# Pooled attention and a gated convolution FFN on one core: masks, fillers, q loads, conv buffers, one batch's pooling and the queue order changed together

## The chip, the cores and the metric

The kernel runs on one core of a Trainium2 chip, in one launch. The metric is the device time in microseconds; for one core this is the time of that core. A profile is taken of one execution, whose own time and span are given below beside the times of the unprofiled runs.

## The reference

Inputs are q, k and v of 8 batches, 8 heads, 576 positions and 64 channels, and the weights of a feed-forward block. k and v are averaged over groups of 8 neighbouring positions, so that each of the 576 queries attends to 72 keys. The attention output, 8 x 64 = 512 channels wide, goes through a projection to 1024 channels, a ReLU, a convolution over three neighbouring positions per channel, a sigmoid gate, and a projection back to 512.

```python
k_p = k.reshape(B, H, Sp, pool, D).mean(axis=3)      # pool = 8, Sp = 72
v_p = v.reshape(B, H, Sp, pool, D).mean(axis=3)
scores = scale * np.matmul(q, k_p.transpose(0, 1, 3, 2))
attn = softmax(scores)
x = np.matmul(attn, v_p)                             # then heads side by side: 8 x 576 x 512
h = np.maximum(x @ w_in, 0.0)                        # 512 -> 1024
conv_out[s] = sum(conv_w[k] * h[s + k - 1] for k in range(3))
gate = 1.0 / (1.0 + np.exp(-conv_out))
out = (h * gate) @ w_out                             # 1024 -> 512
```

## The kernel before

Everything is computed in bf16 with sums in PSUM in f32. The inputs are f32 in memory and are cast by the transfers that load them; all loads are issued from GpSimd (POOL), all stores and the load of the small convolution weights from SyncE (SP).

The work is cut into operations. Each `pl.add(name, engine, duration, fn, ...)` records one: its name, its engine, an estimated duration, the function that issues its instructions, what it reads and writes, and the PSUM slot that it takes or gives back. When all are recorded, `order()` simulates the engines with these estimates and emits the operations in the order of that simulation: at each step it takes the operation that can start first, and among those that an engine could start within 0.02 us of each other the one with the lowest rank. The ranks are a list of integers, `PARAMS["prio"]`, one for each operation in the order in which the operations are recorded. So an engine's order of instructions is fixed when the kernel is built, and an instruction that waits holds back all behind it on that engine; POOL's loads are in that order too. `PARAMS["act"]` names the copies that go to ScalarE (ACT); those not named go to VectorE (DVE).

The operations of batch b, in the order of the data:

- `ldk`, `ldv`, `ldq`: the loads (L440 and L444 for k, L460 and L465 for v, L410 for q). k, v and q have two buffers each, by batch. A row of k_b holds the 8 neighbouring positions of one pooled position, 512 elements.
- `kp1`, `kp2`, `ksum` and `vp1`, `vp2`, `va` (L593, L600, L610, L642): the pooling on DVE, each step adding the two halves of what is left. `vb` (L646, L651) multiplies the pooled v by a mask, which places each head's rows, into `vblk`.
- `qg` (L420): two copies for each batch that regroup q by head pairs. `qT` (L664) transposes q on PE, `qTe` (L670) copies it out of PSUM; `kT` and `kz` (L623, L630) do the same for the pooled k.
- `sc` (L690, L692) the scores, `exp` (L698) their exponential on ACT, `av` (L715, L719) the product with `vblk`, `rc` and `nm` (L728, L732) the division, `xt` (L746) the transpose and `xte` (L752) the copy to `xT`.
- `mm1` (L766 for batch 0, in two parts; L789 for the others) and `relu` (L773, L795): the projection to 1024 channels, in 8 blocks `f` of 128.
- The convolution, for two blocks at a time: mostly on DVE and ACT (`cp0` and `cp2`, L835 on ACT or L837 on DVE, then `ca0` L844 and `ca2` L854), with `cv` as its buffer, of which there are two; five blocks take it on PE (L912) with the diagonal weights `dw` (L562). `tanh` (L862, L919) is the gate, `g` (L900) the product.
- `mm2` (L943) the projection to 512, for pairs of batches in 9 tiles of 128 rows; `oe` (L966) copies a tile out and `st` stores it.

Where the simulation has PE idle in the first 60 us, `warm` (L382) puts filler matmuls on a tile of zeros into the gap, with a count that follows from the gap's simulated length.

Constants come first: `zero` (L483) is the operand of the fillers, `ident` the identity, `mask` the mask for `vb`. Its columns 8 to 12 are built by nine memsets on DVE (L552 to L555), the rest by one memset and two selects on POOL (L542, L547).

Of the kernel before, what the change touches and what calls it, by code (L numbers as in the profile page):

```python
# [17 lines left out]
        "8 1 5 16 3 9 18 19 20 21 56 30 24 23 12 22 37 66 2 185 123 108 153 106 121 104 90 43 "  # L18
        "27 78 117 97 87 114 14 6 77 41 7 11 46 53 0 10 17 29 25 4 13 31 45 51 60 64 107 174 "
        "32 34 50 67 71 55 15 42 35 40 26 38 49 58 48 52 44 47 59 62 69 74 54 73 75 33 63 36 "  # L20
        "57 28 82 61 65 39 86 91 116 88 89 83 100 126 95 92 80 98 99 94 96 70 105 133 76 85 101 112 "
        "140 109 113 93 81 79 72 154 160 164 170 179 175 142 125 137 178 150 161 171 176 68 183 200 202 205 204 184 "
        "190 193 199 201 191 197 203 186 195 207 189 194 221 224 208 210 215 219 216 209 222 225 230 228 226 180 235 243 "
        "242 220 231 236 239 245 115 144 130 134 102 111 136 139 146 156 147 165 172 181 206 227 234 249 84 110 127 128 "
        "120 119 129 118 122 135 132 138 141 151 232 217 246 241 157 163 124 103 145 148 155 158 223 247 196 192 260 264 "
        "280 288 292 298 131 143 152 149 162 167 168 169 238 211 166 182 248 257 261 266 237 240 302 319 341 336 338 327 "
        "370 340 356 382 173 159 198 187 253 314 269 273 301 324 188 213 233 258 218 252 214 229 177 272 281 287 321 290 "
        "365 345 339 335 368 362 354 361 350 347 353 379 387 400 394 381 377 406 389 415 390 395 398 407 420 405 410 414 "
        "421 358 416 422 408 433 441 268 275 262 267 300 299 283 276 285 284 305 303 317 250 254 274 278 265 293 296 308 "
        "279 304 297 329 325 342 244 251 255 271 294 270 315 330 323 331 328 306 349 291 295 282 289 322 316 311 320 344 "  # L30
        "357 380 403 401 418 424 435 442 492 499 496 509 517 518 536 545 561 565 259 256 286 277 326 334 337 359 366 369 "
        "307 309 310 367 318 263 312 348 212 346 351 364 376 372 363 375 402 436 393 360 411 417 355 374 423 431 439 446 "
        "447 444 451 457 511 524 481 487 471 542 546 495 504 466 533 534 513 527 532 539 540 456 467 464 475 488 483 470 "
        "480 460 501 506 510 529 538 440 445 453 459 450 469 458 465 474 482 485 491 505 512 530 544 490 497 560 568 515 "
        "551 520 555 570 592 593 502 521 476 473 526 503 525 486 535 543 553 537 548 541 595 605 603 621 636 627 635 657 "
        "673 666 333 332 352 343 388 396 399 404 413 412 371 385 373 384 378 392 386 391 313 425 427 430 434 429 549 563 "
        "419 426 550 556 516 522 437 443 581 597 596 650 633 615 634 639 655 661 652 659 662 674 677 654 663 669 679 683 "
        "658 675 670 684 685 554 557 572 589 579 588 569 598 587 591 583 614 628 625 564 578 574 586 590 599 566 607 609 "
        "626 638 623 653 688 646 664 584 602 667 642 671 616 681 693 707 698 710 717 601 594 608 618 645 637 651 644 640 "
        "613 660 665 705 714 720 731 730 740 750 760 770 765 771 782 787 802 798 397 409 432 428 454 507 478 484 479 489 "  # L40
        "438 452 449 448 462 461 472 468 383 494 498 508 519 571 604 612 641 648 624 629 528 531 622 631 734 737 739 747 "
        "767 749 758 761 757 775 756 764 772 786 791 769 776 779 785 790 778 792 795 797 801 702 703 643 699 715 711 701 "
        "718 721 713 722 727 743 746 694 700 692 695 708 704 732 725 723 741 733 736 748 806 735 744 729 742 763 738 751 "
        "754 777 783 788 781 809 841 709 716 712 719 753 752 745 762 766 768 774 773 799 832 826 854 842 870 856 861 871 "
        "892 816 907 493 463 500 477 547 552 559 582 585 610 523 514 619 630 558 576 567 575 455 562 577 573 728 690 755 "
        "759 724 726 682 689 672 678 676 668 805 811 813 838 844 840 845 846 873 875 859 864 867 879 887 794 869 865 878 "
        "883 881 882 888 898 902 822 828 815 820 851 818 827 821 831 807 857 843 872 880 804 810 808 814 812 819 825 824 "
        "780 829 833 836 850 848 876 885 852 860 884 868 891 866 905 894 912 917 918 928 817 823 834 839 835 853 830 847 "
        "855 862 901 890 927 910 924 935 939 923 963 944 965 954 996 1006 1018 1032 1038 600 611 617 680 686 697 580 606 649 "
        "656 687 691 632 647 620 696 706 796 793 837 849 858 863 784 789 874 877 800 803 886 895 899 938 949 889 893 896 "  # L50
        "900 903 897 906 911 962 970 941 945 948 956 959 951 958 961 952 969 916 922 921 925 932 930 929 946 934 971 950 "
        "942 960 968 908 914 904 909 915 931 919 920 926 936 940 937 947 953 976 974 913 933 987 957 978 943 980 991 989 "
        "995 998 1002 966 972 955 964 988 984 993 986 994 1016 1003 1017 1023 1025 1027 1036 1034 1044 1047 1039 1040 1052 1055 1056 967 "
        "975 979 982 997 1010 1045 992 1009 1014 1083 1019 1030 1026 1013 1021 973 977 1046 1054 983 1005 990 999 1012 1053 1051 1007 1015 "
        "981 1004 1031 1029 1020 1033 1037 1041 1048 1043 1042 1050 1001 1011 985 1008 1057 1049 1022 1000 1024 1028 1035 1060 1058 1059 1062 1065 "
        "1066 1061 1063 1068 1067 1071 1064 1073 1070 1069 1072 1075 1076 1074 1077 1078 1079 1081 1080 1082 "
# [6 lines left out]
        "kz.0.0 qTe.0.1 qTe.0.3 xte.0.0 xte.0.3 kz.1.1 qTe.1.0 qTe.1.1 xte.1.0 xte.1.1 xte.1.2 xte.1.3 "  # L63
        "xte.1.4 cp0.0.0 cp0.0.1 cp0.0.2 cp0.0.5 cp0.0.6 cp2.0.7 oe.0.0 oe.0.1 oe.0.2 oe.0.3 kz.2.0 "
        "kz.2.1 qTe.2.0 qTe.2.1 xte.2.0 xte.2.2 xte.2.3 xte.2.4 cp2.1.2 cp0.1.7 cp2.1.7 oe.0.4 oe.0.5 "
        "oe.0.6 oe.0.7 oe.0.8 qTe.3.1 qTe.3.2 xte.3.0 xte.3.1 xte.3.2 xte.3.3 xte.3.4 cp0.2.1 cp2.2.2 "
        "cp0.2.5 cp0.2.6 cp0.2.7 cp2.2.7 oe.1.0 oe.1.1 oe.1.2 oe.1.3 kz.4.0 kz.4.1 qTe.4.1 qTe.4.2 "
        "xte.4.0 xte.4.1 xte.4.3 cp0.3.1 cp2.3.1 cp0.3.3 cp2.3.2 cp2.3.7 oe.1.5 oe.1.6 oe.1.7 qTe.5.0 "
        "qTe.5.1 qTe.5.2 xte.5.0 xte.5.2 cp2.4.0 cp2.4.1 cp2.4.3 cp0.4.4 cp0.4.6 oe.2.2 oe.2.3 kz.6.1 "
        "qTe.6.1 xte.6.3 cp0.5.0 cp0.5.2 cp2.5.2 cp0.5.4 cp0.5.5 cp0.5.6 cp0.5.7 cp2.5.7 oe.2.4 oe.2.5 "  # L70
        "oe.2.6 kz.7.0 qTe.7.0 qTe.7.1 xte.7.2 xte.7.3 cp0.6.0 cp2.6.0 cp0.6.3 cp2.6.3 cp0.6.4 oe.3.0 "
        "oe.3.1 oe.3.2 cp0.7.0 cp0.7.3 cp0.7.5 oe.3.5 oe.3.6 oe.3.7 oe.3.8.0 "
# [5 lines left out]
    "acc": [0, 0, 0, 0, 0, 0, 0, 0],  # L78
    "ncv": 2,
# [203 lines left out]
def packets(n, nbytes, cast=True):  # L283
    return n / 16, 0.022 + 0.000074 * nbytes if cast else 0.006 + 0.000038 * nbytes
# [3 lines left out]
def kernel(  # L288
# [86 lines left out]
    def warm(gap, x):  # L375
        n = min(int((gap - 0.05) / 0.06), 100)
        if x is not None:
            t = pp.tile([P, 2 if x[0] == "A" else 1, 512], FP32, name=f"psw{x[0]}", tag=f"ps{x[0]}{x[1]}")[:, 0, 0:P]
        else:
            return  # L380
        for _ in range(n):
            nc.tensor.matmul(out=t, lhsT=zero[:, 0:P], rhs=zero[:, 0:P], start=True, stop=True)  # L382
# [14 lines left out]
    def load_q(b, prio):  # L397
# [6 lines left out]
        n = 2 if b == 0 else 1  # L404
        for x in range(n):
            c = slice(x * H // n, (x + 1) * H // n)
            ys = (x,) if n > 1 else (0, 1)

            def fn(e, c=c):
                nc.gpsimd.dma_start(out=q_b[b % NQ][:, c].rearrange("p h i d -> p h (i d)"), in_=rows_q(b)[:, c, :])  # L410
            pr = prio + (PARAMS["ld0"][x] if b == 0 else 0.0)
            pl.add(f"ldq{b}.{x}", "POOL", 0.8, fn, writes=[("ql", b % NQ, y) for y in ys], prio=pr, dma=packets(PR * H // n, 1024))
# [68 lines left out]
    def consts():  # L481
        def fn(e):
            nc.vector.memset(zero, 0.0)  # L483
        zi = pl.add("zero", "DVE", 0.15, fn, writes=["zero"], prio=-80)

        def fn(e):
            make_identity(nc, ident)
# [581 lines left out]
```

## Time and profile before

| | |
|---|---|
| median of the runs | 212.78 us |
| lowest and highest of 3 runs | 212.31 and 214.05 us |
| the profiled execution | 214.0 us, span 212.3 us |
| mean granted clock of PE | 0.992 |
| PE busy, with fillers | 199.2 us |
| fillers on PE (L382) | 19.3 us |
| DVE busy | 181.3 us |
| ACT busy | 174.2 us |
| POOL busy | 45.2 us |
| loads issued from POOL | 16.80 MB in bf16 |

The busy time of an engine is the time in which it executes; the share is taken of the span, from the first instruction to the last. The time of an execution is a little longer than its span. The transfers of a queue run on 16 DMA engines; "landing" is the time from a transfer's issue until its data is there. Idle time that the profile gives to a releaser ended when that releaser finished.

### The profile page before, as it was taken

What the parts mean: (1) busy time and instruction counts of PE and PEld (TensorE: products, weight loads), DVE (VectorE), ACT (ScalarE), POOL (GpSimd) and SP (SyncE); (2) the same over time, 40 slices, a digit from 0 to 9 for tenths busy, and PEclk for the clock granted to TensorE, in tenths of its full rate; (3) what the DMA queues carried; (4) which work ended last, traced back from release to release, by engine and by line L of the source; (5) the groups of instructions that cost most, each with busy time, mean ns of one, the idle gap of its engine ahead of it and who ended that gap; (6) DMA issues with size and microseconds to landing.
All of it is one profiled execution on the core that took longest, in us unless ns stands there. A gap on an engine that the chain in (4) does not pass through costs nothing.

```text
span 212.3 us, 4770 instructions
## 1 busy us (share of the span) xinstructions
PE 199.2 (94%) x1900; PEld 136.7 (64%) x1900; DVE 181.3 (85%) x419; ACT 174.2 (82%) x297; POOL 45.2 (21%) x73
## 2 busy tenths in 40 slices
PE   3999996979997799999999999999999999999993
PEld 3997784857753557756865676756656847764541
DVE  5446889899999999999999999999999978997510
ACT  2017388999999988999999999988999998998412
POOL 7695299602233223130000000000000000000000
PEclk9999999799999999999999999999999999999999
DMA  4999999999999999999302020122020203002344
GB/s 59 178 197 205 207 198 202 203 207 172 199 159 202 227 223 159 221 137 176 114 3 98 5 99 0 54 99 99 3 98 1 102 32 116 3 2 99 147 154 148
DMA packets 26363, 26.56 MB, mean 125 GB/s; under 512 B 5708, under 2 KB 21348, under 8 KB 26340
## 3 DMA queue, kind: packets, MB, share of 16 engines
q0 software_dynamic: 21200, 16.80, 50.8%
q1 hardware_dynamic: 5140, 9.45, 11.8%
q8 instruction: 15, 0.25, 0.4%
q14 instruction: 8, 0.07, 0.1%
HBM read 33.57 MB, written 9.44 MB: 203 GB/s over the span
## 4 chain that ended last, share of the span: by engine, by line
PE 76%; DVE 14%; ACT 6%; issue 2%
PE psfB L943 25%; PE psfA L789 22%; PE pswA L382 6%; PE psfA L715 4%; PE psfA L690 3%; PE psbB L746 3%; PE psbB L664 2%; PE pswB L382 2%; DVE cv L837 2%; PE psfA L719 2%; DVE cv L844 2%; ACT tg L862 2%; DVE p L593 1%; ACT hT L795 1%; DVE cv L854 1%
## 5 line engine op out<-in xcount | busy, mean ns | idle before, releaser
L943 PE MATMUL psfB<-w_out,gT 128*128 128x512 bf16 (+1 forms) x282 | 65.2, 377 | 0.0
L789 PE MATMUL psfA<-xT,w_in 128*128 128x288 bf16 x448 | 59.7, 286 | 0.7 <-ACT xT L752 0.7
L789 PEld LDWEIGHTS <-w_in 128*128 128x128 bf16 x448 | 42.4, 98 | 12.8 <-issue 0.9
L943 PEld LDWEIGHTS <-gT 128*128 128x128 bf16 x290 | 27.7, 98 | 28.8 <-issue 0.3
L795 ACT ACTIVATE hT<-psfA 128x576 bf16<-128x576 f32 x56 | 35.8, 665 | 2.8 <-PE psfA L789 2.8
L835 ACT ACTIVATE cv<-hT,cr 128x576 bf16<-128x576 bf16 x41 | 31.9, 792 | 0.2
L837 DVE TENSOR_SCALAR cv<-hT,cr 128x576 bf16<-128x576 bf16 x77 | 27.8, 381 | 2.3 <-ACT tg L862 0.9
L732 DVE TENSOR_TENSOR xx<-psfA,rr 128x512 bf16<-128x512 f32 (+1 forms) x40 | 26.9, 680 | 0.1
L900 DVE TENSOR_TENSOR gT<-tg,hT 128x1152 bf16<-128x1152 bf16 x32 | 23.8, 746 | 3.1 <-ACT tg L862 1.8
L698 ACT ACTIVATE attnT<-psfA 128x576 bf16<-128x576 f32 x40 | 25.2, 673 | 1.5 <-PE psfA L690 1.1
L844 DVE TENSOR_TENSOR cv<-cv,hT 128x1152 bf16<-128x1152 bf16 (+1 forms) x32 | 22.4, 703 | 2.3 <-ACT cv L835 2.2
L862 ACT ACTIVATE tg<-cv,cs 128x576 bf16<-128x576 bf16 x29 | 22.1, 799 | 0.6 <-DVE cv L854 0.6
L854 DVE TENSOR_TENSOR cv<-cv 128x1152 bf16<-128x1152 bf16 (+1 forms) x32 | 22.5, 702 | 0.1
L862 ACT ACTIVATE tg<-cv,cn 128x576 bf16<-128x576 bf16 x30 | 22.4, 784 | 0.1
L670 ACT COPY qT<-psbB 128x792 bf16<-128x792 bf16 (+2 forms) x12 | 9.6, 814 | 13.3 <-PE psbB L664 13.3
L382 PEld LDWEIGHTS <-zero 128*128 128x128 bf16 x243 | 17.0, 111 | 4.9 <-DVE zero L483 3.5
L966 ACT COPY osb<-psfB 128x512 f32<-128x512 f32 x26 | 15.4, 598 | 4.8 <-PE psfB L943 4.7
L382 PE MATMUL pswA<-zero 128*128 128x128 bf16 x182 | 13.9, 245 | 3.5 <-DVE zero L483 3.5
L690 PE MATMUL psfA<-qT,kz 128*128 128x512 bf16 x64 | 13.4, 301 | 2.9 <-ACT kz L630 1.3
L715 PE MATMUL psfA<-vblk,attnT 128*128 128x130 bf16 (+1 forms) x160 | 15.8, 222 | 0.3
L715 PEld LDWEIGHTS <-attnT 128*128 128x128 bf16 (+1 forms) x160 | 11.0, 100 | 4.4 <-issue 1.3
L746 PEld LDWEIGHTS <-xx 128*128 128x128 bf16 (+1 forms) x160 | 9.5, 97 | 6.1 <-DVE xx L732 2.6
(91 smaller groups left out, 265.7 us busy)
## 6 DMA issues: line engine op xcount, KB each, us to landing
out_dram<-osb SPq DMA_DIRECT2D x14, 512.0 KB, 2.8
k_b<-in_k_dram POOLq DMA_DIRECT2D x8, 512.0 KB, 10.3
q_b<-in_q_dram POOLq DMA_DIRECT2D x7, 576.0 KB, 12.1
v_b<-in_v_dram POOLq DMA_DIRECT2D x7, 512.0 KB, 11.8
out_dram<-osb SPq DMA_DIRECT2D x7, 256.0 KB, 2.1
v_b<-in_v_dram POOLq DMA_DIRECT2D x8, 128.0 KB, 7.5
w_in<-in_moe_w_in_dram POOLq DMA_DIRECT2D x1, 1024.0 KB, 10.1
w_out<-in_moe_w_out_dram POOLq DMA_DIRECT2D x2, 512.0 KB, 10.9
```

Source lines behind the costliest of these rows:

```text
L382: nc.tensor.matmul(out=t, lhsT=zero[:, 0:P], rhs=zero[:, 0:P], start=True, stop=True)
L698: nc.scalar.activation(out=attnT[m][:, t, :], in_=slot(key).rearrange("p i x -> p (i x)")[:, 0:S], func=ACT.Exp, scale=1.0 / 64.0)
L715: nc.tensor.matmul(out=a[0:n, g, c * w:(c + 2) * w], lhsT=attnT[m][:, s, u0:u0 + n], rhs=vblk[m][:, 2 * s:2 * s + 2, :].rearrange("p x d - ...
L732: nc.vector.tensor_tensor(out=xx[i3][0:n].rearrange("p (g h e) -> p g h e", g=2, h=4), in0=av_view()[:, :, :, 0:D], in1=rr[i3][0:n].rearra ...
L789: nc.tensor.matmul(out=t[:, i, 0:HC], lhsT=w_in[:, c, f * P:(f + 1) * P], rhs=xT[m][:, c, i * HC:(i + 1) * HC], start=(c == 0), stop=(c == ...
L795: nc.scalar.activation(out=h_(b)[:, f, hs(b), 2:S + 2].rearrange("p (i x) -> p i x", i=2), in_=slot(key)[:, :, 0:HC], func=ACT.Relu)
L835: nc.scalar.activation(out=cv[y][:, kk // 2, z0:z1, :], in_=src, func=ACT.Copy, scale=sc)
L837: nc.vector.tensor_scalar(out=cv[y][:, kk // 2, z0:z1, :], in0=src, scalar1=sc, scalar2=None, op0=OP.mult)
L844: nc.vector.tensor_tensor(out=cv[y][:, 0, 0:n, :], in0=cv[y][:, 0, 0:n, :], in1=h_at(2), op=OP.add)
L854: nc.vector.tensor_tensor(out=cv[y][:, 0, 0:n, :], in0=cv[y][:, 0, 0:n, :], in1=cv[y][:, 1, 0:n, :], op=OP.add)
L862: nc.scalar.activation(out=tg[i3][:, zs[z0]:zs[z0] + z1 - z0, :], in_=cv[y][:, 0, z0:z1, :], func=ACT.Tanh if half else ACT.Sigmoid, scale ...
L943: nc.tensor.matmul(out=a[:, 0, j0:j1], lhsT=g[:, c, t * P:(t + 1) * P], rhs=w_out[:, c, j0:j1], start=(c == 0), stop=(c == n_fb - 1), skip ...
```

## The change

- The masks: `zero` and the other first memsets stay on DVE, but the nine memsets for the columns 8 to 12 of the mask are replaced by two selects on POOL, and the memset on POOL covers all 12 columns.
- The fillers: a gap g gets int((0.93 g - 0.2) / 0.058) of them instead of int((g - 0.05) / 0.06).
- q: each batch is loaded by two transfers, of 64 and of 8 partitions, with all heads. Before, batch 0 was loaded by two transfers of four heads, the others by one, each of 72 partitions. A regroup waits for both.
- `ncv`: three conv buffers instead of two.
- `acc`: for batch 2, k and v are loaded in two steps. A first transfer brings the first 256 elements of each row, a second adds the other 256 to them on the way; `kp1` and `vp1` of this batch fall away. The second transfer waits for the first.
- The durations that the simulation uses for some operations and transfers are others, and the ranks and the list of copies on ACT are new. Four regroups of q (both of batch 1, one of batch 4, one of batch 6) are on ACT now.

```diff
-    "ncv": 2,
+    "ncv": 3,
-    "acc": [0, 0, 0, 0, 0, 0, 0, 0],
+    "acc": [0, 0, 1, 0, 0, 0, 0, 0],
...
-def packets(n, nbytes, cast=True):
-    return n / 16, 0.022 + 0.000074 * nbytes if cast else 0.006 + 0.000038 * nbytes
+def packets(n, nbytes, cast=True, engines=16):
+    return n / engines, 0.003 + 0.0000765 * nbytes if cast else 0.004 + 0.000034 * nbytes
...
-        n = min(int((gap - 0.05) / 0.06), 100)
+        n = min(int((0.93 * gap - 0.2) / 0.058), 100)
...
-        n = 2 if b == 0 else 1
-        for x in range(n):
-            c = slice(x * H // n, (x + 1) * H // n)
...
+        for x, (r0, r1) in enumerate(((0, 64), (64, PR))):
+            def fn(e, r0=r0, r1=r1):
+                nc.gpsimd.dma_start(out=q_b[b % NQ][r0:r1].rearrange("p h i d -> p h (i d)"), in_=rows_q(b)[r0:r1])
+            pl.add(f"ldq{b}.{x}", "POOL", 0.8 - 0.2 * x, fn, writes=[("ql", b % NQ, x)], prio=prio, dma=packets((r1 - r0) * H, 1024))
...
-            nc.gpsimd.memset(mask[:, 0:8, :], 1.0)
...
-            nc.vector.memset(mask[:, 8:12, :], 0.0)
-            for c in range(4):
-                nc.vector.memset(mask[32 * c:32 * c + 32, 8 + c, :], 1.0)
-                nc.vector.memset(mask[32 * c:32 * c + 16, 8 + c, :], 0.0)
+            nc.gpsimd.memset(mask, 1.0)
...
+        for x, (m_, base, sg, st_) in enumerate(((mk[:, 0], Sp - 1, -1, 0), (mk[:, 1], -Sp, 1, 0), (rem, -16, 1, -32), (rem, 31, -1, 32))):
+            def fn(e, m_=m_, base=base, sg=sg, st_=st_):
+                nc.gpsimd.affine_select(out=m_, in_=m_, compare_op=OP.is_ge, fill=0.0, base=base, pattern=[[st_, 4], [0, D + 1]], channel_multiplier=sg)
```

The ranks of the first loads on POOL, read from the two lists (an operation's place in the list is its place in the order of recording):

```
before: k 0, 10   q 4, 13    v 17, 25, 29   w_in 31   q of batch 1 44       k of batch 1 45, 51
after:  k 6, 9    q 15, 19   v 21, 26, 32   w_in 50   q of batch 1 35, 41   k of batch 1 67, 92
```

The copies on ACT, counted from the two lists (batches 0 to 3, batches 4 to 7; `oe` by pairs of batches, 0 and 1, 2 and 3):

```
        before           after
cp      20, 21           18, 17
qTe      8,  8            6,  8
kz       4,  4            3,  7
xte     16,  8           11, 10
qg       0,  0            2,  2
oe      16, 12           17, 11
```

## The prediction

> **What bounds the kernel now.** I read the page first: busy shares, then the row of slices.
>
> ```profile
> span 212.3 us, 4770 instructions
> PE 199.2 (94%) x1900; PEld 136.7 (64%) x1900; DVE 181.3 (85%) x419; ACT 174.2 (82%) x297; POOL 45.2 (21%) x73
> ...
> PE   3999996979997799999999999999999999999993
> DVE  5446889899999999999999999999999978997510
> ACT  2017388999999988999999999988999998998412
> ...
> DMA  4999999999999999999302020122020203002344
> ```
>
> PE looks full, but its share counts the fillers of L382, which compute nothing. The busy time by stretch separates the stages. Columns: stretch, length, busy us of PE, weight loads, DVE, ACT, POOL, granted clock, DMA share, GB/s.
>
> ```profile
> 17.40:24.50 7.10, 7.10 (x104) 5.49 (x101) 5.48 (x18) 3.41 (x6) 2.13 (x4) 1.00 1.21 204
> ...
> 34.00:47.40 13.40, 10.24 (x134) 7.40 (x131) 12.58 (x30) 12.48 (x22) 6.42 (x9) 0.87 1.24 205
> ...
> 60.00:76.60 16.60, 13.80 (x153) 8.20 (x149) 16.52 (x38) 16.48 (x28) 5.79 (x8) 1.00 1.10 204
> 76.60:208.80 132.20, 132.09 (x1099) 85.61 (x1099) 117.24 (x260) 117.96 (x197) 5.35 (x7) 1.00 0.35 88
> ```
>
> From 76.6 us to 208.8 us PE has no idle time, nor fillers: that stretch is the PE's own work, and only less work could shorten it. Fillers come to 19.3 us in all (groups of L382: 13.9 on pswA, 5.4 on pswB), so the real PE work is 199.2 - 19.3 = 179.9 us, and 212.3 - 179.9 = 32.4 us of the span are lost. Nearly all lies ahead of 76.6 us, with 3.5 us behind the last matmul. So the question is how much sooner the work before 76.6 us can be fed. The timeline shows three causes: the start, batch 1, and DVE and ACT being nearly full.
>
> ```profile
> 8.01 5.68 PE L382 MATMUL pswA<-zero 128*128 128x128 bf16 x88
> 9.41 0.75 DVE L420 COPY q<-q_b 72x2048 bf16<-72x2048 bf16 x1
> 14.63 0.70 DVE L420 COPY q<-q_b 72x2048 bf16<-72x2048 bf16 x1
> 15.25 0.47 DVE L610 TENSOR_TENSOR ksum<-p 128x640 bf16<-128x640 bf16 x1
> 20.60 0.40 PE L715 MATMUL psfA<-vblk,attnT 128*128 128x130 bf16 x4
> 24.50 0.82 PE L766 MATMUL psfB<-xT,w_in 128*128 128x384 bf16 x4
> 31.99 0.91 DVE L593 TENSOR_TENSOR p<-k_b 128x1280 bf16<-128x1280 bf16 x1
> 36.33 0.42 PE L690 MATMUL psfA<-qT,kz 128*128 128x512 bf16 x2 [1.31 <-ACT kz L630]
> ```
>
> Start: the first half of q is regrouped by 10.2 us, yet PE runs 88 fillers to 13.5 us before it transposes it; DVE, waiting for that transpose, comes to the second half of q (landed at 4.04 + 7.6 = 11.6 us) and to ksum only at 14.6 and 15.3 us. The attention output matmuls start at 20.6 us, the first expert matmul 3.9 us later, at 24.5 us. Batch 1: its k landed at 26.2 us (below), but is pooled at 32.0 us, and its scores come at 36.3 us. Between 34.0 and 47.4 us PE loses 3.2 us idle, 2.6 us in fillers, and about 1.2 us because the clock is halved from 36.9 to 40.3 us while some 2.4 us of real work runs: 7.0 us.
>
> The list of transfers gives issue to landing:
>
> ```profile
> w_in<-in_moe_w_in_dram POOLq DMA_DIRECT2D x1, 1024.0 KB, 10.1
> q_b<-in_q_dram POOLq DMA_DIRECT2D x1, 576.0 KB, 12.1
> k_b<-in_k_dram POOLq DMA_DIRECT2D x1, 512.0 KB, 13.6
> ```
>
> Issued at 9.67, 11.71 and 12.61 us, they land at 19.8, 23.8 and 26.2 us. All move about 205 GB/s together from 4.5 us on, so in the first 30 us a landing follows from the bytes queued ahead of it.
>
> **The change, part by part.**
>
> *Start.* The new ranks put batch 1's q (35, 41) ahead of w_in (50); before, w_in (31) came ahead of it (44). In bf16 the bytes up to w_in's end are k 0.59, q 0.59, v 0.66, q of batch 1 0.59, w_in 1.05: 3.47 MB instead of 2.88 MB. Fast bound: 0.14 MB have moved by 4.5 us, 3.33 MB at 205 GB/s take 16.2 us, and 1.0 us to the landing (before, the windows had moved 0.2 MB beyond w_in's place by then): 21.7 us. Slow bound: the same bytes as the old queue had at the end of q, 23.8 us. The attention ahead of it gains time: DVE no longer builds a mask (9 memsets, 0.93 to 2.71 us) before it zeroes the filler operand, so the fillers start at about 1.3 instead of 3.5 us, and the first block, 39 fillers of 111 ns, no longer holds the conv-weight transpose to 7.8 us (and with it the POOL queue 1.8 us, L562). A gap g gets (0.93g - 0.2)/0.058 fillers for (g - 0.05)/0.06: 35 for 39 in a gap of 2.4 us, 4 x 0.06 to 0.11 = 0.2 to 0.4 us less to overrun, in the same path. With all of q at about 11 us, two regroups of 0.7, transposes, five exps of 0.57, the outputs can start at 16 to 17 us and finish near 21: w_in is then the last to come. Against it, both regroups of batch 1 move to ACT. No row shows one there. ACT copies take 0.639 us for 576 and 0.852 us for 792 elements, 1 ns each, so 2048 take 2.1 us (bounds 0.71 as on DVE, 2.8 by the 0.79 us for 576 of L835). Queued between the exps and the xT copies they cost up to 4.2 us. I take the first expert matmul at 23.0 us: **-1.5 us** (bounds -2.8 by w_in's fast landing; +1.9 as worked out in the second rival).
>
> [...]
>
> *Issue cost on POOL.* Seven more q issues at 0.55 us (the row of k's short part) are 3.9 us, and two more mask selects (0.73) and a longer memset (0.3) 1.8 us, on an engine idle 79%. In the start w_in's issue moves from 9.7 to about 11.9 us, hidden by the transfers queued ahead, which last until about 17; without that cover it would be 2.2 us. I take 0.
>
> [...]
>
> *Batch 1.* k lands when it did (the same 4.06 MB are ahead: 25 to 26.5 us), v one q later (0.59 MB, 2.9 us: 32 us). But q's regroups (DVE, 1.5 us at 26.7 us), its transposes (PE 1.4 us) and copies now lie in the wait for w_in, so k can be pooled sooner than 32.0 us. Of the 7.0 us lost I take **-1.5 us**, what leaves DVE ahead of k; bounds 0 and -5.5, the 32.0 - 26.5 us that k waits.
>
> *DVE and ACT.* Batch 2's first pooling steps become accumulating transfers: two of 0.81 us leave DVE, -1.6. By the lists, DVE gets in the batches 0 to 3 two cp, two qTe, five xte, one kz and gives two qg and one oe: +2.0 us; ACT there loses 1.8 us, in spite of the two regroups. In batches 4 to 7 ACT gains 2.8 us (two qg of 2.1, three kz, two xte, less four cp and one oe), DVE loses 0.9. The third conv buffer removes at most the 0.9 us of DVE copies waiting for ACT's L862. Within 80 to 180 us ACT is idle 3.5 us, so the 2.8 us just fit; without that room they would cost 2.8. I take **-0.2 us**, bounds -2.5 and +2.8.
>
> The accumulating transfer is in no row. At best it costs its bytes, which stay 0.59 MB for k (twice half a row): 0. At worst its second part only starts when the first has landed and POOL stands still meanwhile: another 12.4 us on k's landing at 38.9 us. k is pooled at 48.1 and batch 2's scores come only at 63.9 us. I take 0, nearest the plain loads; the bound is the third rival.
>
> Sum: -1.5 - 1.5 - 0.2 = **-3.2 us**. The profiled execution took 214.0 us (212.3 of span, 1.7 around), so 210.8; it is 1.2 us above the median of the runs, 212.78, so the median forecast is **209.6 us**.
>
> **Rivals.** (1) *Hidden anyway.* w_in lands at 23.8 us, and what the start still wins is lost behind DVE (98% busy from 30 to 160 us) or the fuller ACT. For it: those shares, and bytes that do not shrink. Against it: 7 us lost around batch 1 are waits, not work. Time: -0.7 at the start and the rest given back, 212.1 us.
>
> (2) *Slower: the ACT regroups hold the start.* Place: ACT between batch 0's exps and xT copies. By the old landings 2.42 MB are in at 17.6 us; a regroup ends at 19.7, the last exp at 20.3, outputs to first expert matmul 4.0 us as now, and the second regroup among the xT copies 2.1: 26.4 us, +1.9. PE, out of fillers, would then run its next 3.4 us at half clock as at 36.9 us, +1.7. 212.8 + 3.6 = 216.4 us. It decides once q lands after 15.7 us with both regroups in the path (15.7 + 2.1 + 0.6 + 4.0 + 2.1 = 24.5). Against it: ACT has little else to do from 20.7 to 25.3 us now, and the exps may go first.
>
> (3) *The accumulating chain is late.* With two waits of 12.4 us k of batch 2 lands at 38.9 + 24.8 = 63.7 us, plus 3.5 us from pooling to scores as in batch 1 (32.0 to 36.3, less the 0.8): 67.2 against 63.9 us, +3.3: 216.1 us. It decides past 60 us; two waits in a row are unlikely since POOL has time to issue early.
>
> **Numbers.** Forecast 0.60, rival 1 0.23, rival 2 0.12, rival 3 0.05. A measurement of this kernel tells about 1% from no change (its runs span 212.31 to 214.05). So faster 0.60, same 0.23, slower 0.17. Range: down to 206.0 us (start -2.8, batch 1 -3.8, -0.2), up to 214.6 us, which takes in rival 1 and the start alone at +1.9; beyond lie most of rivals 2 and 3.
>
> **What would show it.** Right: the filler operand zeroed by about 1.3 us; the first expert matmul (L766's successor) at 22 to 24 us, just behind w_in's landing; batch 1's scores before 35 us; PE full from about 73 us to about 205. Wrong: w_in landing after 24 us; ACT in a regroup while an exp or xT copy is due; PE idle or half-clocked between 80 and 200 us; batch 2's second k part landing after 60 us.

## The result, and the profile after

The changed kernel takes 223.32 us in the median of four runs (221.06 to 225.51) against 212.79 us before; the ratio is 1.045, 95% interval 1.035 to 1.055. One of the four, the profiled execution of 225.51 us, is in a slower state (mean granted clock 0.967, the others 0.976 to 0.984), so the ratio and all differences below leave out such runs: 222.58 us, the median of the other three, is 9.8 us above the kernel before. The forecast was 209.6 us, the range 206.0 to 214.6. The trace is read here for order and kind, and the sizes are taken from the medians of the runs.

Page of the changed kernel, busy shares and slices (each digit 5.6 us):

```profile
span 223.8 us, 4717 instructions
PE 203.4 (91%) x1872; PEld 136.5 (61%) x1872; DVE 180.0 (80%) x413; ACT 175.9 (79%) x292; POOL 53.7 (24%) x86
...
PE   8867799789899759979999999999999999999993
...
PEclk9979669999999996999999999999999999999998
DMA  4999999999999999999100021112202201202243
GB/s 72 169 191 168 167 183 180 173 171 155 185 178 158 219 196 236 223 223 192 17 0 3 0 94 55 44 47 97 94 3 94 94 3 47 94 3 95 94 189 141
```

DVE and ACT have as much to do as before (181.3 and 174.2 us there). What is new is a dip of PE in slices 14 and 15 (73 to 84 us), a clock below full at 22 to 34 us (0.72 in the mean), and a rate of 155 to 191 GB/s in most of the first 73 us, where the kernel before moved about 200; the DMA row stays busy to 106 us. Stretches of the changed kernel (start:end, length, busy us of PE, weight loads, DVE, ACT, POOL, granted clock, DMA share, GB/s):

```profile
17.40:27.10 9.70, 7.22 (x104) 6.03 (x103) 7.71 (x21) 5.37 (x6) 8.84 (x18) 0.85 1.23 172
25.00:31.00 6.00, 6.00 (x47) 4.30 (x46) 1.99 (x4) 2.94 (x7) 3.85 (x7) 0.50 1.16 164
34.00:50.00 16.00, 13.60 (x203) 10.61 (x201) 15.53 (x36) 15.56 (x29) 13.11 (x15) 1.00 1.40 179
50.00:80.00 30.00, 26.76 (x229) 16.84 (x227) 24.77 (x54) 25.43 (x41) 13.11 (x18) 1.00 1.21 179
80.00:100.00 20.00, 15.63 (x137) 8.56 (x136) 13.40 (x34) 12.55 (x20) 5.45 (x8) 0.91 1.23 222
100.00:220.20 120.20, 119.56 (x989) 78.58 (x986) 106.16 (x238) 106.95 (x179) 0.00 (x0) 1.00 0.21 66
```

From 80 to 100 us, where PE had no gap before, it is now busy 15.63 of 20 us, with DVE and ACT at two thirds: all three wait for data. From 100 us on it is full again. In order of time:

```profile
0.89 0.11 DVE L479 MEMSET zero<- 128x64 uint32 x1 [0.89 <-PEq L1044]
21.11 3.70 ACT L416 COPY q<-q_b 72x2048 bf16<-72x2048 bf16 x2 [3.27 <-DMA q_b<-in_q_dram]
24.71 0.57 ACT L743 COPY xT<-psbB 128x512 bf16<-128x512 bf16 x1
27.05 1.46 PE L757 MATMUL psfA<-xT,w_in 128*128 128x384 bf16 x4
38.95 0.42 PE L681 MATMUL psfA<-qT,kz 128*128 128x512 bf16 x2 [0.29 <-DVE kz L621]
59.98 0.49 DVE L591 TENSOR_TENSOR p<-k_b 128x640 bf16<-128x640 bf16 x1 [3.32 <-DMA k_b<-in_k_dram]
```

The filler operand is zeroed at 0.89 us, as forecast. But q of batch 1 lands at 21.1 us, its two regroups hold ACT to 24.8, an xT copy of batch 0 waits behind them, and the first expert matmul comes at 27.05 us, not 23.0; batch 1's scores come at 38.95, not before 35. The list of transfers: w_in, issued at 10.18, takes 15.9 us and lands at 26.1, against 10.1 and 19.8 before.

```profile
w_in<-in_moe_w_in_dram POOLq DMA_DIRECT2D x1, 1024.0 KB, 15.9
```

The chain that ended last, which had no DMA step of 2% before, now spends 25% of the span on DMA. Its pieces around the dip:

```profile
50.89 17.78 DMA q_b<-in_q_dram
68.66 0.29 issue
68.95 13.23 DMA q_b<-in_q_dram
82.18 0.02 issue
82.20 0.69 DVE q L416
```

A q transfer takes 17.8 us, a later one is issued only when it has landed, and that one comes to DVE at 82.2 us with nothing left to do ahead of it.

### The profile page after: what moved, and what is told of

Its sections match the earlier page's. It is cut to its first block, busy times and chain, and to the rows that moved or that the text cites. A ratio compares the mean times of both kernels' runs of the same rounds, so it can differ in the third digit from the quotient of the medians.

```text
span 223.8 us, 4717 instructions
## 1 busy us (share of the span) xinstructions
PE 203.4 (91%) x1872; PEld 136.5 (61%) x1872; DVE 180.0 (80%) x413; ACT 175.9 (79%) x292; POOL 53.7 (24%) x86
## 4 chain that ended last, share of the span: by engine, by line
PE 49%; DMA 25%; ACT 15%; POOL 4%; DVE 3%; issue 2%; ACTq 0%; POOLq 0%
PE psfB L934 22%; DMA q_b<-in_q_dram 19%; PE psfA L780 15%; DMA v_b<-in_v_dram 6%; ACT hT L786 4%; ACT tg L853 3%; ACT cv L826 2%; PE psfA L706 2%; ACT attnT L689 2%; PE psbB L737 2%; PE psfA L681 2%; ACT q L416 2%; POOL k_b L436 1%; PE psfA L710 1%; PE psbA L737 1%
## 5 line engine op out<-in xcount | busy, mean ns | idle before, releaser
L934 PE MATMUL psfB<-w_out,gT 128*128 128x512 bf16 (+1 forms) x282 | 66.6, 383 | 0.2
L780 PEld LDWEIGHTS <-w_in 128*128 128x128 bf16 x448 | 42.9, 98 | 14.5 <-issue 3.6
L828 DVE TENSOR_SCALAR cv<-hT,cr 128x576 bf16<-128x576 bf16 x83 | 29.0, 374 | 6.5 <-ACT hT L764 3.9
L826 ACT ACTIVATE cv<-hT,cr 128x576 bf16<-128x576 bf16 x35 | 26.9, 796 | 0.1
L723 DVE TENSOR_TENSOR xx<-psfA,rr 128x512 bf16<-128x512 f32 (+1 forms) x40 | 26.4, 677 | 0.2
L853 ACT ACTIVATE tg<-cv,cn 128x576 bf16<-128x576 bf16 x30 | 22.4, 779 | 3.1 <-DVE cv L845 1.9
L835 DVE TENSOR_TENSOR cv<-cv,hT 128x1152 bf16<-128x1152 bf16 (+1 forms) x32 | 22.3, 701 | 0.9 <-ACT cv L826 0.8
L845 DVE TENSOR_TENSOR cv<-cv 128x1152 bf16<-128x1152 bf16 (+1 forms) x32 | 22.3, 701 | 0.1
L957 ACT COPY osb<-psfB 128x512 f32<-128x512 f32 x27 | 16.1, 597 | 6.9 <-PE psfB L934 5.1
L661 ACT COPY qT<-psbB 128x720 bf16<-128x720 bf16 (+2 forms) x10 | 7.3, 765 | 11.2 <-PE psbB L655 11.2
L383 PEld LDWEIGHTS <-zero 128*128 128x128 bf16 x215 | 14.1, 106 | 2.6 <-DVE zero L479 1.1
L737 PEld LDWEIGHTS <-xx 128*128 128x128 bf16 (+1 forms) x160 | 10.3, 100 | 6.9 <-DVE xx L723 3.1
L655 PEld LDWEIGHTS <-q 72*128 72x128 bf16 x256 | 10.4, 102 | 5.7 <-DVE q L416 2.7
## 6 DMA issues: line engine op xcount, KB each, us to landing
w_in<-in_moe_w_in_dram POOLq DMA_DIRECT2D x1, 1024.0 KB, 15.9
```

What stands on the lines that cost most here:

```text
L723: nc.vector.tensor_tensor(out=xx[i3][0:n].rearrange("p (g h e) -> p g h e", g=2, h=4), in0=av_view()[:, :, :, 0:D], in1=rr[i3][0:n].rearra ...
L780: nc.tensor.matmul(out=t[:, i, 0:HC], lhsT=w_in[:, c, f * P:(f + 1) * P], rhs=xT[m][:, c, i * HC:(i + 1) * HC], start=(c == 0), stop=(c == ...
L826: nc.scalar.activation(out=cv[y][:, kk // 2, z0:z1, :], in_=src, func=ACT.Copy, scale=sc)
L828: nc.vector.tensor_scalar(out=cv[y][:, kk // 2, z0:z1, :], in0=src, scalar1=sc, scalar2=None, op0=OP.mult)
L835: nc.vector.tensor_tensor(out=cv[y][:, 0, 0:n, :], in0=cv[y][:, 0, 0:n, :], in1=h_at(2), op=OP.add)
L845: nc.vector.tensor_tensor(out=cv[y][:, 0, 0:n, :], in0=cv[y][:, 0, 0:n, :], in1=cv[y][:, 1, 0:n, :], op=OP.add)
```

## The experiments

My theory after the first trace: the transfers of 64 partitions slow the loads, and the accumulating batch adds waits. Its rival: the new order, with GpSimd waiting in it, is at fault and the cut is harmless. The first four runs undo one thing each.

**q whole** (the changed kernel with one transfer of 72 partitions for each q):

```
-  for x, (r0, r1) in enumerate(((0, 64), (64, PR))): ... dma_start(out=q_b[..][r0:r1], in_=rows_q(b)[r0:r1])
+  dma_start(out=q_b[b % NQ].rearrange(..), in_=rows_q(b))
```

> The changed kernel with every batch's q loaded by one transfer of 72 partitions again, at the place of the 64-partition one; all else and the order of all other instructions as changed. Theory S (the loads of 64 and 8 partitions make the transfers slower): the rate in the first 50 us is back near 200 GB/s from some 170, w_in lands by 24 us instead of 26.1, and the time is 216 us or less against 223. Theory A (the two-step loads of batch 2 are late and hold the queue): the start is a little better, but batch 2's second v part still lands near 70 us and the time stays above 219 us. Theory Q (the new order puts q of later batches ahead of w_in, k and v): landings keep their order, the time stays above 219 us.

Measured 216.45 us, ratio 1.018 (1.014 to 1.023). The cut costs 6.1 us (6.9 by the median of all four runs, the figure that some expectations below name), the greater part of the loss. w_in lands at 24.7 us, later than the 24 expected. Most of the dip goes too; the same stretch here:

```profile
80.00:100.00 20.00, 18.95 (x210) 13.61 (x209) 17.69 (x43) 16.25 (x28) 3.42 (x5) 1.00 1.10 206
```

**Batch 2 not accumulated** (loaded whole, with its first pooling steps on DVE again), first beside the cut, then with q whole:

```
-  k and v of batch 2: columns 0:256, then columns 256:512 with accum_op=add
+  k and v of batch 2: columns 0:512; vector.tensor_tensor(p1 = src[.., 0:256] + src[.., 256:512])
```

> The changed kernel with batch 2's k and v loaded whole by the first transfer, the second left out, and the two first pooling steps (0.81 us each) back on DVE ahead of the second ones; q in 64 and 8 partitions, order as changed. Theory A: k and v of batch 2 are there by 45 us instead of 60 and 70, and the time falls to 216 us or less. Theory S: the slow packets at 16 to 20 us remain and w_in lands near 26 us; 219 to 222 us. Theory Q: 219 to 222 us as well.

> Both of the above: q by one transfer, batch 2 loaded whole; masks, fillers, third conv buffer and the order of instructions as changed. If S and A hold all of the loss, 213 us or less. If the order itself (theory Q) costs more than 2%, 217 us or more, with PE still idle somewhere between 20 and 100 us behind a k, v or w_in that lands later than before.

Measured 220.01 us (1.033, 1.029 to 1.038) and 216.33 us (1.016, 1.011 to 1.021). Beside the cut the accumulating batch costs 2.6 us by the medians, and the intervals overlap; with q whole it costs nothing (216.45 against 216.33). So the two do not seem to be additive. With both undone 3.5 us remain, between the two expectations.

**The cut alone, in the kernel before:**

```
-  dma_start(out=q_b[b % NQ][:, c], in_=rows_q(b)[:, c, :])
+  for r0, r1 in ((0, 64), (64, PR)): dma_start(out=q_b[b % NQ][r0:r1, c], in_=rows_q(b)[r0:r1, c, :])
```

> The kernel before with each q transfer cut into 64 and 8 partitions, issued one after the other at the old place (9 issues become 18); all else as before. Theory S: the transfers slow as in the changed kernel, 217 us or more. Theories A and Q: the loads have 10 us of slack from batch 1 on, so 212 to 215 us.

Measured 212.99 us, 1.001 (0.998 to 1.004). The same cut is free under the old order. Its trace has slow stretches as well (150 GB/s at 29 to 34 us, 202 without the cut), w_in lands at 21.6 and not 19.8, and yet the first expert matmul (24.31 us) and the end do not move: those loads had slack there. So neither theory holds alone. The cut slows loads, and the new order is what makes that cost time.

**Is the transfer of 64 partitions slow by itself?** Only transfers, nothing computed:

```
whole: dma_start(q_b[0:72])          cut: dma_start(q_b[64:72]); dma_start(q_b[0:64])
```

> This kernel only loads, in five stretches, each ended by a read of what was loaded, and computes nothing of the reference. A: four batches of q, 72 partitions in one transfer each. B: the same as 64 and 8 partitions. C: q, w_in, q, k, q, k with q in 72. D: the same with q in 64 and 8. E: four batches of k, 128 partitions. Theory 1 (the transfer of 64 partitions makes every packet in the queues slower): a packet of 1024 bytes takes about 98 ns in A, C and E and 160 to 210 ns in B and, while q runs, in D; w_in's packets of 2048 bytes about 173 ns in C and 250 to 300 in D; B and D move 140 to 165 GB/s, A, C and E 190 to 210. Theory 2 (the packets were slow because of what else ran on the chip's engines in those stretches, not because of the cut): with nothing else running all packets of 1024 bytes take about 98 ns in every stretch, and B is no slower than A.

The issues of its stretches overlapped, so they can't be compared as wholes; but from 24 to 31 us, with cut transfers on their way, the packets of 1024 bytes took 98 ns (median of each us) at 199 to 208 GB/s, and from 12 to 17 us, mostly whole ones, 107 to 170 ns at 132 to 200. Theory 1 as stated there fell. The next run kept the stretches strictly apart:

> Only transfers, none of the reference computed; stretches strictly in turn, each twice, with no engine at work beside them: four batches of q in 72 partitions; the same as 8 and 64; three times q in 72 and four tiles of k in 128; the same with q as 8 and 64. The earlier run of transfers alone had slow packets both in a stretch of 72 and in one of 64 and 8, so it did not tell the cut from the pairing of neighbours. If the cut alone makes packets slow, both stretches with it have many 1024-byte packets over 130 ns (10% and more) and move under 185 GB/s, in both repeats, and the others do not. If slow packets come from which transfers lie side by side, they turn up in stretches of either kind, or only in the mixed ones. If they need the engines at work, they turn up in none.

Duration, rate and share of 1024-byte packets that took over 130 ns, counted from the packets of the trace, in the two repeats:

```
four q, whole            16.1 us  147 GB/s  31%      16.1 us  146 GB/s  29%
four q, cut              14.3     165        3%      14.4     164        4%
three q and k, whole     20.9     160        3%      21.6     155        9%
three q and k, cut       18.6     179        3%      18.1     185        3%
```

Alone, the cut is faster, in every pair: the opposite of the kernel. Then the loads of the kernel's first 35 us, close to the changed kernel's order and still with no engine at work on what they bring:

> Only transfers, none of the reference computed: the loads of the changed kernel's first 35 us in its order (k, q, v of batch 0, q of batch 1, w_in, k of batch 1, q of batch 2, v of batch 1, q of batch 3, k of batch 2), four times in turn, q whole, cut, whole, cut. Four transfers of q in a row had slow packets when whole and none when cut, in both repeats, so the cut alone is not what slows them. If the company of w_in, k and v does it, the stretches with the cut show packets of 150 ns and more while q of batch 1 and w_in are in flight and take 3 us and more longer than the others, as in the kernel. If the engines at work beside the loads are needed for it, the cut stretches take as long as the whole ones or 1 to 3 us less.

Whole, cut, whole, cut:

```profile
30.80:66.30 35.50, 0.00 (x0) 11.64 (x22) 1.00 1.12 183
72.50:109.50 37.00, 0.00 (x0) 14.40 (x33) 1.00 1.22 175
114.60:151.00 36.40, 0.00 (x0) 12.71 (x29) 1.00 1.11 178
156.10:193.90 37.80, 0.00 (x0) 14.45 (x33) 1.00 1.18 172
```

The cut stretches take 1.4 to 1.5 us longer and keep the DMA engines busier (last but one column) for the same bytes. The packets that took over 1.3 times their usual time (98 ns for 1024 bytes, 173 for 2048) are 1.6% of all in both whole stretches, 18.8% and 15.6% in the cut ones. From a stretch's first issue, q of batch 1 lands after 17.3 us whole and 18.8 and 19.0 cut, w_in after 22.3 and 22.2 whole, 23.1 and 24.1 cut. So no engine is needed for the slow packets: they come with the cut in the company of k, v and w_in, with other partition counts and packet sizes. The delay is 1 to 2 us, less than the 3 us expected and much less than the kernel loses. And it is not all theirs: GpSimd, with two more issues, comes to w_in's issue 1.8 us later in the cut stretches (7.1 and 7.0 us after the first issue, against 5.3 and 5.2).

**Two transfers, or the 64 partitions?**

```
-  enumerate(((0, 64), (64, PR)))
+  enumerate(((0, 36), (36, PR)))
```

> The changed kernel with each q cut into 36 and 36 partitions, not 64 and 8: as many transfers and GpSimd issues. If the loss of the cut (6.9 us) comes from the transfer of 64 partitions and how its packets fall on the 16 DMA engines, this runs like the uncut one: 216 to 218.5 us. If it comes from having two transfers for each q (a further issue of 0.6 us on GpSimd and a further wait), it stays at 221 to 224.

Measured 217.02 us, 1.020 (1.015 to 1.024), as with q whole: the further issue on GpSimd is free. What costs is the cut into 64 and 8. The slow packets go with it: of the 1024-byte packets of the first 75 us 11.8% took over 130 ns in the changed kernel, 1.9% with q whole, 2.8% in 36 and 36, 1.5% in the kernel before. No run tells the 64 from the 8, but in the changed kernel the 8 of batch 1 had landed at 17.6 us and packets stayed slow to 20 us, which points to the 64.

**Where in the kernel?** Cut in batches 0 and 1 alone, then only from batch 2 on:

```
+  if b < 2:   (the counterpart: b >= 2)   two transfers, 64 and 8;   else one of 72
```

> The changed kernel with q cut into 64 and 8 partitions in batches 0 and 1 alone, the other six whole (cut nowhere it took 216.4 us, cut everywhere 223.3). If the cut costs at the start (w_in and q of batch 1 late), 220 to 223 us. If it costs in the loads of batches 2 and 3, where GpSimd is held up, 216.5 to 218.5 us.

> The counterpart: q whole in batches 0 and 1, cut from batch 2 on. If the cut costs at the start, 216.5 to 218.5 us. If it costs in the loads of batches 2 and 3, 220 to 223 us. If the two places add up, this and the counterpart lie together about 7 us above twice 216.4.

Measured 219.10 us (1.031, 1.023 to 1.038) and 219.83 us (1.034, 1.029 to 1.039): 2.7 and 3.4 us over the 216.45 with q whole, together 6.0 of the 6.1, which was the third outcome named. A delay of 1 to 2 us in the start becomes 2.7, and the later ones cost somewhat more.

**The half clock.** Fillers where PE waits for batch 1's regroups:

```
+  if b == 1: 14 x nc.tensor.matmul(out=t[..], lhsT=zero[:, 0:P], rhs=zero[:, 0:P])   ahead of each q transpose
```

> The changed kernel with 14 filler matmuls ahead of each of batch 1's three q transposes, where PE waits for the regroups on ACT. If the half clock of 25 to 31 us is a cost of its own (my rival 2 of the prediction), the clock there rises from 0.50 to near 1 and the kernel gains 1.5 to 3 us: 220.3 to 221.8 us. If PE is ahead of its data there anyway, because the loads behind set the pace, the clock rises and the time stays at 222.5 to 224.

Measured 222.50 us, 1.043 (1.037 to 1.050). The clock from 25 to 31 us is 1.00 instead of 0.50, and the median is 0.1 us lower, which the intervals separate neither from nothing nor from a gain of 1 to 2 us. It is no clean price of the half clock either: the regroups end at 24.5 us, but the last block of fillers ends at 26.4, and the first expert matmul comes at 27.18 us, no earlier than without them, though w_in has landed at 25.0.

**The other parts in the old order:** masks on GpSimd, the new filler count, the third conv buffer.

```
+  memset(mask, 1.0) and four affine_select on GpSimd;   n = int((0.93 * gap - 0.2) / 0.058);   cv[n_off % 3]
```

> The kernel before with three parts of the change and its own order: the mask of the remainder built on GpSimd, the new count of fillers, the third conv buffer. If the loss is all in the loads (cut, accumulating batch, order), it runs as before: 212.0 to 213.5 us. If one of these parts has a cost (GpSimd's selects delaying its load issues, fillers that run into the first transposes), 214 us or more. If the third buffer is worth what the sum allowed it, 210.5 to 212.

Measured 212.99 us, 1.001 (0.998 to 1.004). They cost nothing in the old order. But they gain nothing either, though the first expert matmul comes 2.7 us earlier than the 24.5 us before:

```profile
21.82 0.81 PE L766 MATMUL psfB<-xT,w_in 128*128 128x384 bf16 x4
```

**Short filler blocks** in the old order, with the masks on GpSimd, blocks up to 60, up to 40, and up to 60 with the third buffer:

```
-  n = min(int((gap - 0.05) / 0.06), 100)
+  n = min(int((gap - 0.05) / 0.06), 60)      (then 40; then 60 and cv[n_off % 3])
```

> The kernel before with the mask of the remainder on GpSimd and no filler block longer than 60 (one of 88 is cut to 60), so that PE is free when q of batch 0 has landed. The first expert matmul should come 1 to 2 us earlier (22.5 to 23.5 us), w_in landing at about 19.8 as before. If a start gained is kept to the end, 210.8 to 211.8 us; if the later loads take it back, 212.3 to 213.3.

> The kernel before with the mask of the remainder on GpSimd and no filler block over 40 (60 took 211.7 us, first expert matmul 22.4 us). If an earlier start is kept to the end about half, as there, a start 0.5 us earlier gives 211.2 to 211.7; if PE is now held by q of batch 0 (landed 12.0 us) and not by its fillers, the same 211.4 to 212.1.

> The same with blocks up to 60 and the third conv buffer. The kernel with the new count, the masks and the third buffer began its expert matmuls at 21.8 us, 2.7 earlier than before, and gained nothing (213.0); this one has only the short blocks in place of the new count. If the third buffer takes back what the start gains, 212.7 to 213.5 us; if it is free, 211.4 to 212.1 us and the new count is what differed.

Measured 211.71 us (0.991, 0.989 to 0.994; 211.46 to 212.04, four runs), 211.92 us (0.996, 0.992 to 1.001; 210.46 to 214.15, ten runs) and 213.07 us (1.001, 0.997 to 1.004). The first is the fastest of all, 1.4 us ahead of the kernel before in the same set of runs (213.11), two thirds of the 2.1 us by which its first expert matmul is earlier (22.4 us); the second, whose interval just takes in 1, does not confirm it with certainty. The third buffer brought nothing here and may have taken the gain back: I leave that open.

**The rest of 3.5 us: the new order.** It is put down to the new ranks and the new list for ACT by elimination: the masks, the fillers and the third buffer cost nothing in the old order, and were not taken out of the new one. It need not be lost at the start: with q in 36 and 36 w_in lands at 23.4 us and the first expert matmul comes 0.4 us earlier than in the kernel before, but between 80 and 100 us PE is idle for 1.9 us:

```profile
24.12 0.82 PE L757 MATMUL psfA<-xT,w_in 128*128 128x384 bf16 x4
80.00:100.00 20.00, 18.12 (x199) 12.56 (x197) 18.07 (x46) 15.94 (x28) 4.40 (x6) 1.00 1.12 208
```

The chain that ended last spends 34% of the span on DMA with q whole and 22% with both undone. To the kernel with q whole and batch 2 not accumulated: w_in ahead of q of batch 1, then batch 1's regroups on DVE, then both. Each time the simulation gave a new order of the other operations too, so none of the three changes one thing alone.

```
rank of w_in 50 -> 41, of q of batch 1 41 -> 50;      -  "act": "qg.1.0 qg.1.4"
```

> The changed kernel with q whole in 72 partitions and batch 2 not accumulated (that one took 216.3 us), and w_in issued ahead of q of batch 1 on GpSimd. If the 3.4 us that this version still loses to the kernel before come from w_in queued behind q of batch 1, w_in lands 2 to 3 us earlier (about 21.5 to 22.5 us), the first expert matmul comes at about 23 us and the kernel takes 213 to 214.5 us. If they come from batch 1's q landing and its regroups on ACT, which would only get later, 216 to 218 us.

> The changed kernel with q whole and batch 2 not accumulated (216.3 us), and batch 1's two regroups on VectorE (0.68 us each) in place of ScalarE (1.85 us each), where they keep the xT copies of batch 0 waiting. If that wait sets the first expert matmul (24.8 us there, 0.5 us after w_in), the matmul moves little, to 24.4, because w_in holds it too, and the kernel gains at most 1 us: 215 to 216.5 us. If the ScalarE time itself is short later, 213.5 to 215.

> The same with w_in issued ahead of q of batch 1, which with the regroups on ScalarE took 224.3 us. If that loss came from the regroups on ScalarE (24.6 to 28.3 us, the expert epilogues behind them), it falls to 214 to 218 us here. If it came from q of batch 1 landing 5 us later and the loads behind it, it stays at 221 to 224.

Measured 224.27 us (1.054, 1.049 to 1.059), 221.39 us (1.041, 1.036 to 1.046) and 223.82 us (1.049, 1.043 to 1.054). The first two missed what either theory gave; the third is where the later landing of q of batch 1 and the loads behind it would put it, which speaks against the regroups on ACT as the cause of the first. With w_in first it lands at 20.4 us and the first expert matmul comes at 23.13, what I had forecast for the change; but q of batch 1 lands at 24.4 and is regrouped after that:

```profile
23.13 0.81 PE L764 MATMUL psfB<-xT,w_in 128*128 128x384 bf16 x4
24.62 3.70 ACT L417 COPY q<-q_b 72x2048 bf16<-72x2048 bf16 x2
28.76 0.48 PE L662 MATMUL psbA<-ident,q 72*128 72x72 bf16 x10 [1.89 <-ACT hT L771]
```

and from 34 to 50 us PE waits 3.4 us for one regroup, which waits for a q that was issued at 28.6 and landed at 43.5. An early first matmul was worth nothing here, where later loads moved back. With the regroups on DVE, w_in is issued at 9.3 us and lands at 25.1; what else costs 5 us there I did not settle, nor which part of the new order the 3.5 us come from.

## Why the prediction was wrong

**Start: -1.5 us forecast, first expert matmul at 23.0; measured 27.05.** The step that failed is the term of w_in's landing: bounds of 21.7 and 23.8, measured 26.1, and 24.7 with q whole. It rests on two readings, 205 GB/s from 4.5 us on, and a landing that follows from the bytes queued ahead. From 4.5 us to w_in's landing the queue moved 180 GB/s (189 with q whole); in the kernel before it was 193 over that part, so the 205 came from a later stretch. And 4.02 MB had come in by then, not 3.47 (3.96 with q whole), as loads issued behind w_in moved beside it; in the old order it was 3.07 for 2.88. The rows of the changed kernel from 0 to 26.1 us and of the kernel before from 0 to 19.8 us (packets, MB, share of 16 engines):

```profile
q0 software_dynamic: 4749, 4.02, 106.9%
q0 software_dynamic: 3381, 3.07, 96.4%
```

I had no row with a transfer of 64 partitions among others and carried the rate of other shapes over to it. With q alone the cut moves more than the whole transfers (165 and 164 against 147 and 146 GB/s), with q and k as well (179 and 185 against 160 and 155), and in the company of the kernel's loads less (175 and 172 against 183 and 178). Four cut transfers alone had only 3 to 4% slow packets, so the cut by itself is no sufficient cause. Why company slows them stays open: no run here shows the cause.

**Rival 2** named the mechanism next to it: batch 1's regroups on ACT (1.85 us each, inside my 0.71 to 2.8) do hold the xT copies, from 21.1 to 24.8 us, and the granted clock is 0.50 after, from 25 to 31 us. The chain of the profiled execution comes to the first expert matmul over q of batch 1, these regroups and the transposes behind them, not over w_in, which had landed 0.95 us before; with batch 2 whole w_in landed at 24.6 us and the matmul came at 26.03. So the regroups held the start too, which my sum did not count as a term of its own, and rival 2's 26.4 us for that matmul was near. But it counted q landing by 17.6, not 21.1 us. Its price of the half clock, 1.7 us, was not tested cleanly. That the half clock is free is not shown: of the ten runs with blocks up to 40 those at a mean clock of 1.000 took 210.6 to 211.5 us and those at 0.984 took 212.9 to 213.3. Its total, 216.4 us, is near that of q whole by chance.

**Batch 1: -1.5 us.** It got none. Its scores come 2.6 us later than before, the same 2.6 us that the first expert matmul is late. I had k land when it did, at 25 to 26.5 us, and v at 32: measured 29.6 and 38.9. Part of it lies in the new order of GpSimd's issues. Behind w_in comes a part of batch 2's v, which has to wait until batch 0's v is pooled, and k of batch 1 is issued behind it, at 18.85 us instead of 12.61:

```profile
18.13 0.73 POOL L461 DMA_DIRECT2D v_b<-in_v_dram  x1 [6.31 <-DVE p L584]
```

With q whole and batch 2 not accumulated the wait is still 6.0 us, k lands at 27.2 and v at 34.2. What the wait costs by itself no run shows.

**DVE and ACT: -0.2 us.** The busy times moved little, as forecast (DVE 1.3 us less, ACT 1.7 more on the page). Whether the term was right is not shown: the chain that ended last runs over ACT for most of 100 to 129 us, 15% of the span in all against 6% before, and no run changed this part alone.

**Issues on GpSimd: 0**, and right: the masks in the old order and the cut into 36 and 36 cost at most 0.6 us.

**The accumulating transfer: 0, rival 3 at 0.05.** A batch accumulated cost 0.1 us with q whole and 2.6 beside the cut, the latter not clear of the scatter. Of batch 2's second parts k landed at 59.9 us, just inside my bound, but v, which I had not priced at all, at 70.0. The term was priced by itself, and seems to depend on whether the loads around it are late.

**The premise that failed most** is the reading of the first table: "from 76.6 us to 208.8 us PE has no idle time", taken as the PE's own work. It was so because, in the old order, the loads landed ahead of their use. The same cut costs nothing there and 6.1 us in the new order. I priced each part for the moment at which it is issued, and no part for the slack of the transfers behind it.

**What was called wrong beforehand came:** w_in after 24 us, ACT in a regroup while an xT copy was due, PE idle between 80 and 100 us.

## What to carry to other kernels

Before a load is split or moved, list for each transfer behind it when it lands and when it is first read: a shape that was harmless where loads landed ahead of their use (212.99 us, ratio 1.001) cost 6.1 us here, more than its own delay of 1 to 2 us, where they did not. A transfer rate read from one mix of shapes did not hold for another (193 GB/s up to w_in's landing before, 180 after), and the shape measured alone pointed the wrong way (four q 14.3 us cut against 16.1 whole, the kernel's loads 37.0 and 37.8 against 35.5 and 36.4); it has to be measured in the order in which the kernel issues it. Nor did w_in's landing follow from the bytes queued ahead alone (4.02 MB had come in by then, not 3.47): ask also what is issued behind and moves beside it. In these runs a stage that started earlier gained nothing where the loads of the next stages came later (first expert matmul at 23.13 us, 224.27 us in all).

## What was not expected of the hardware

- q in transfers of 64 and 8 partitions came faster than in transfers of 72 when loaded alone (four batches in 14.3 and 14.4 against 16.1 us) and slower among k, v and w_in (37.0 and 37.8 against 35.5 and 36.4 us), with no engine at work.
- Four whole q in a row had 29 to 31% slow packets (1024 bytes, over 130 ns), and far fewer when k lay between them (3 and 9%).
- In the changed kernel the packets of w_in (2048 bytes) took 265 to 311 ns (median of each us from 16 to 20) while q of batch 1 was on its way, against 173 otherwise: what slows is not only the cut transfer itself.
- In the changed kernel ACT regrouped 72x2048 elements in 1.9 us, DVE in 0.68 (medians 1898 and 684 ns).
